# Attention numerator of a linear-attention and Fourier-mixing kernel: whole-array products on head-major features in place of products on column halves

## The chip, the cores and the metric

The kernel runs on one core of a Trainium2 chip. The metric is the device time of one execution in microseconds, as the median of several runs. The profile is of one execution of its own; its times start at the first instruction of that execution.

## The reference: what is computed

There are two blocks. The first is an attention with random features, over 8 batches, 8 heads, 576 positions and a head size of 64, with 128 features. For each batch and head:

```
phi(x) = exp(h - max(h)) / sqrt(128),  h = x omega^T - |x|^2 / 2   (x scaled by 64^(-1/4))
kv = phi(k)^T v                 128 x 64
z  = sum over positions of phi(k)
num = phi(q) kv,   den = phi(q) z + 1e-6
attn = num / den                576 x 64
```

The heads are joined to rows of 512. The second block adds to these rows x the real part of a two-dimensional Fourier transform over positions and columns, u = x + Re(FFT2(x)), normalizes each row of u, and returns u + relu(un w_ch1) w_ch2 with a hidden size of 2048. The two weight matrices arrive as 64-bit floats.

## The kernel before, in words

**Tiling of the attention.** Heads are taken in pairs, so there are 32 pairs (8 batches by 4). The 576 positions of a head are 64 x 9: partition p and chunk r (R = 9 chunks) hold position 9p + r. One tile thus has 128 partitions, 64 for each head of the pair. `attn` (from L407) does a pair:

- it transposes nine 128 x 128 tiles of k and q together (`transposed`, L354, tile `kqT`), and forms the projections `pp` (L433);
- `softmax` (L382) takes the maximum over features on VectorE (L387) and the exponential on ScalarE (L399). The resulting feature tiles `e` have (head, position) on partitions;
- `kvp` (L455) is the sum over nine chunks of features of k by v, with a column of ones for the denominator, so that each head has 65 columns. VectorE copies it to `kv` (L467);
- the features of q are transposed in the groups of chunks (0), (1 to 4), (5 to 8), each into one PSUM bank, and ScalarE copies each group to the tile `qeT` (L378): 128 features on partitions, and for each chunk 128 columns, head 0's 64 positions and then head 1's. The copy of the last group reads each 128 columns backwards, which also swaps the heads in them;
- the numerator products write `ndp`, two PSUM banks: 65 columns for each of four slots in the first bank (head 0), and for four slots and two more in the second (head 1, and chunk 0 of both heads). Each of the slots holds two chunks: the dictionary `SLOTS` (L28) says for chunks 1 to 8 which half of the output partitions and which slot each takes. A product at L496 has a stationary piece of 128 features by 64 positions and writes 64 output partitions, so that it uses a column half of TensorE's array. The two products at L504 have 128 stationary columns, of which the first 64 outputs are used later;
- VectorE adds a small number to the denominators (L517), takes reciprocals (L520) and multiplies (L527) into the batch's tile `x`.

The rest of a batch is `mix` (folds on VectorE L552 to L566, transforms `yp` L591 and `ab` L618 and L623 on TensorE), then norms, and for four row tiles the plain two-layer product `plain_of` (`hp` L799, `op` L822), while the weights are converted to 32 bit (`narrow`). These are interleaved with the attention. After that, eight blocks of 512 rows go through a fast matrix multiplication with seven products (`first_of` L953, `second_of` L1043).

**What sets the order of the work.** Everything is written as streams of steps (`Step`: engine, planned microseconds, what it waits for, buffers taken and given). `Listing.run` simulates the streams with these planned costs and issues the instructions of a step when it is the earliest that can start. The order of instructions on each engine is therefore fixed when the kernel is built, and the planned costs shape it. The numerator's step on TensorE is planned at 1.5 us, takes two of eight PSUM banks, waits for `kv` and all three copies of `qeT`, and gives back `qeT` and `kv`. The VectorE step after it gives back the two banks.

Of the kernel before, what the change touches and what calls it, by code (L numbers as in the profile page):

```python
# [13 lines left out]
AF = mybir.ActivationFunctionType  # L14
ALU = mybir.AluOpType
AX = mybir.AxisListType
F32 = mybir.dt.float32
# [7 lines left out]

SLOTS = {1: (0, 0), 2: (1, 0), 3: (0, 1), 4: (1, 1), 8: (0, 2), 7: (1, 2), 6: (0, 3), 5: (1, 3)}  # L28
SLOTS[0] = (0, 4)
NL = 2  # L30
NC3 = NL + 1

# [1 line left out]
PE, ACT, DVE, POOL, SP, NONE = "pe", "act", "dve", "pool", "sp", "none"  # L34
# [128 lines left out]
def kernel(  # L163
# [10 lines left out]
    nc = tc.nc  # L174

    B, H, S, D = q.shape
# [12 lines left out]
    P = 128  # L189

    R = S // 64
# [32 lines left out]
    att = early.enter_context(tc.tile_pool(name="att", bufs=NS))  # L224
# [4 lines left out]
        bank=8, kq=NKQ, turned=NS, e=NE, e1=NS, kv=NS, x0=1, x1=1, fold=1, half=1, y=1,  # L229
# [3 lines left out]
    def bank(name):  # L233
        return psum.tile([128, 512], F32, name=name, tag="bank")
# [116 lines left out]
            rows = slice(D * i, D * i + D)  # L351
            nc.vector.tensor_scalar(om2[rows, i, :], omps[rows, 0:128], SCALE, None, op0=ALU.mult)

    def transposed(src, name, groups, after, makes, give, back=None):  # L354


        dst = None
        for j0, j1 in groups:
            m = j1 - j0
            yield Step(  # L360
                PE,
                0.11 * m,
                after=after(j0, j1),
                take=("bank",) + (("turned",) if j0 == 0 else ()),
                give=give(j0, j1),
            )
            if dst is None:
                dst = att.tile([128, R, 128], F32, name=name, tag="turned")
            ps = bank("tps")
            for j in range(j0, j1):  # L370
                nc.tensor.transpose(ps[:, (j - j0) * 128 : (j - j0 + 1) * 128], src(j), ident[:])  # L371
            yield Fork(evicted(dst, ps, j0, j1, makes, (j0, j1) == back))
        return dst

    def evicted(dst, ps, j0, j1, makes, back):
        yield Step(ACT, 0.15 + 0.115 * (j1 - j0), 0.1, makes=makes + (j0,), give=("bank",))
        ps = ps[:, 0 : 128 * (j1 - j0)].rearrange("q (c p) -> q c p", p=128)
        nc.scalar.activation(  # L378
            out=dst[:, j0:j1, :], in_=ps[:, :, ::-1] if back else ps, func=AF.Copy
        )  # L380

    def softmax(n, t, num, ps, es):  # L382

# [23 lines left out]
    def attn(n):  # L407
        b, pr = divmod(n, NP)

        yield Step(NONE, after=(("kq", n), "om2") + ((("vd", n - 1),) if n else ()))  # L410
        kq = kqs.pop(n)

        flat = kq[:].rearrange("p c d -> p (c d)")
        kqT = yield from transposed(
            lambda j: flat[:, 128 * j : 128 * j + 128],
            "kqT",
            ((0, 4), (4, 8), (8, R)),
            lambda j0, j1: (),
            ("kqT", n),
            lambda j0, j1: ("kq",) if j1 == R else (),  # L420
        )
        es = {}
        for t, num in enumerate((4, 4, 4, 4, 2)):
            yield Step(
                PE,
                0.215 * num,
                after=(("kqT", n, 2 * t // 4 * 4),),
                take=("bank",),
                give=("turned",) if num == 2 else (),
            )  # L430
            ps = bank("pp")
            for j in range(num // 2):
                nc.tensor.matmul(  # L433
                    ps[:, 256 * j : 256 * j + 256],
                    lhsT=kqT[:, 2 * t + j, :],
                    rhs=om2[:].rearrange("p i m -> p (i m)"),
                )
            yield Fork(softmax(n, t, num, ps, es))

        def feature(c):  # L440
            return es[c // 4][:, c % 4, :]

        kvp = None
        for r0, r1 in ((0, 4), (4, 8), (8, R)):
            yield Step(
                PE,
                0.225 * (r1 - r0),
                after=(("e", n, r0 // 4),) + (("vd", n),),
                take=("bank",) if r0 == 0 else (),
                give=("e" if r1 < R else f"vd{n % NV}",),  # L450
            )
            if kvp is None:
                kvp = bank("kvp")
            for r in range(r0, r1):
                nc.tensor.matmul(  # L455
                    kvp[:, 0 : 2 * (D + 1)],
                    lhsT=feature(r),
                    rhs=vds[n % NV][:, r, :],
                    start=(r == 0),
                    stop=(r == R - 1),  # L460
                )
        kvs = []

        def keep():
            yield Step(DVE, 0.3, take=("kv",), give=("bank",), makes=("kv", n))
            kv = att.tile([128, 2, D + 1], F32, name="kv", tag="kv")
            nc.vector.tensor_copy(  # L467
                out=kv[:].rearrange("m i d -> m (i d)"), in_=kvp[:, 0 : 2 * (D + 1)]
            )
            kvs.append(kv)  # L470

        yield Fork(keep())

        qeT = yield from transposed(
            lambda r: feature(R + r),
            "qeT",
            ((0, 1), (1, 5), (5, R)),
            lambda j0, j1: tuple(("e", n, t) for t in range((R + j0) // 4, (R + j1 - 1) // 4 + 1)),
            ("qeT", n),
            lambda j0, j1: {1: (), 5: ("e",), R: ("e", "e1")}[j1],  # L480
            (5, R),
        )
        yield Step(
            PE,
            1.5,
            after=(("kv", n), ("qeT", n, 0), ("qeT", n, 1), ("qeT", n, 5)),
            take=("bank", "bank"),
            give=("turned", "kv"),
        )
        ndp = [bank("ndp"), bank("ndp")]  # L490

        for i, order in enumerate(((2, 1, 4, 3, 7, 8, 5, 6), (2, 1, 4, 3, 7, 8, 5, 6))):
            for r in order:
                g, slot = SLOTS[r]
                c0 = D * (1 - i if r >= 5 else i)
                nc.tensor.matmul(  # L496
                    ndp[i][D * g : D * g + D, (D + 1) * slot : (D + 1) * (slot + 1)],
                    lhsT=qeT[:, r, c0 : c0 + D],
                    rhs=kvs[0][:, i, :],
                )  # L500

        flat = qeT[:].rearrange("q c p -> q (c p)")
        for i in range(2):
            nc.tensor.matmul(  # L504
                ndp[1][:, (D + 1) * (4 + i) : (D + 1) * (5 + i)],
                lhsT=flat[:, D * i : D * i + P],
                rhs=kvs[0][:, i, :],
            )
        yield Step(DVE, 1.8, after=(("frame", b),), give=("bank", "bank"), makes=("x", b, pr))
        x = xts[b % 2]  # L510
        rden = small.tile([P, 10], F32, name="rden", tag="rden")
        nds = [
            t[:, 0 : (D + 1) * n].rearrange("p (c d) -> p c d", d=D + 1)
            for t, n in zip(ndp, (4, 6))
        ]
        for i, n in enumerate((4, 6)):
            nc.vector.tensor_scalar(  # L517
                rden[:, 4 * i : 4 * i + n], nds[i][:, :, D], DEN_EPS, None, op0=ALU.add
            )
        nc.vector.reciprocal(out=rden[:], in_=rden[:])  # L520
        cols = x[:, :, 2 * D * pr : 2 * D * (pr + 1)].rearrange("p c (i d) -> p c i d", i=2)
        for p1, dst, nd, den in (
            (P, cols[:, 0:4, 0], nds[0], rden[:, 0:4]),
            (P, cols[:, 0:4, 1], nds[1][:, 0:4], rden[:, 4:8]),
            (64, cols[0:64, 4], nds[1][0:64, 4:6], rden[0:64, 8:10]),
        ):
            nc.vector.tensor_tensor(  # L527
                out=dst,
                in0=nd[:, :, 0:D],
                in1=den.unsqueeze(2).to_broadcast(list(dst.shape)),  # L530
                op=ALU.mult,
            )
# [341 lines left out]
    def pairs(start):  # L874
        for n in range(start, B * NP, NS):
            yield from attn(n)
# [24 lines left out]
        bank=8, slab=0, u=2, ht=NFC, hs=HF, ur=4, s=6, set=2,  # L901
# [241 lines left out]
```

## Time and profile before

| | |
|---|---|
| median of 3 runs | 1330.62 us (1330.33 to 1332.33) |
| the profiled execution | 1329.76 us, span of its instructions 1328.0 us |
| granted TensorE clock, mean | 0.995 |
| instructions | 20075, of which 7777 on TensorE |
| numerator products on column halves (L496) | 1024 MATMUL instructions, 28.5 to 454.0 us |
| numerator products on the whole array (L504) | 128 MATMUL instructions, 29.6 to 454.6 us |
| projections `pp` (L433) | 576 MATMUL instructions |
| copies to `qeT` (L378) | 96, median 592 ns |

A float32 product appears as two MATMUL instructions, each with a weight load (LDWEIGHTS, shown as PEld). "128*64" beside a matmul means 128 rows and 64 columns of the array in use, "128x65" its output of 65 columns in the moving direction. Lengths of matmuls overlap, so that the difference of starts tells what one costs when many follow each other. In lines with "<-" the left side waits for the right one.

### The profile page before, as it was taken

The page shows a single profiled execution, that of the slowest core. Times are in us where ns is not written, and L with a number is a line of the kernel's source. Part 1 is how long each engine was busy: PE and PEld are TensorE (multiplying, and loading weights), DVE is VectorE, ACT ScalarE, POOL GpSimd, SP SyncE. Part 2 cuts the span into 40 slices and gives each one's busy share as a digit, 9 for nine tenths or more (in the row PEclk, how much of TensorE's full clock was granted, in tenths as well). Part 3 has the DMA queues.
Part 4 walks back from the last instruction along what each step waited for, and adds up shares of the span by engine and source line. Part 5 has one row for each costly group of instructions (what it writes and reads, how often), then busy time and mean ns, then how long its engine had stood idle before and what let it go on. Part 6 is the DMA issues. An engine that isn't in the chain of part 4 may idle for free.

```text
span 1328.0 us, 20075 instructions
## 1 busy us (share of the span) xinstructions
PE 1302.6 (98%) x7777; PEld 1135.3 (85%) x7777; DVE 558.1 (42%) x1347; ACT 407.1 (31%) x1200; POOL 294.3 (22%) x407
## 2 busy tenths in 40 slices
PE   5999999999999999899999999999999999999998
PEld 5988988889989776788888888888888888888887
DVE  2788879897575620652132132132131231241211
ACT  4856666565655411210210210210210210210210
POOL 2213222321000010340330340340340330330420
PEclk8999999999999999999999999999999999999999
DMA  8535663554322120100200200200200201101101
GB/s 218 155 108 155 180 175 118 140 167 133 87 92 68 60 76 17 56 17 8 72 17 8 72 17 9 72 17 9 71 17 16 64 17 24 57 16 25 40 1 32
DMA packets 82464, 89.66 MB, mean 68 GB/s; under 512 B 42944, under 2 KB 51392, under 8 KB 82368
## 3 DMA queue, kind: packets, MB, share of 16 engines
q1 hardware_dynamic: 77760, 71.59, 20.0%
q0 software_dynamic: 4608, 16.78, 4.0%
q8 instruction: 62, 1.02, 0.3%
q14 instruction: 34, 0.28, 0.1%
HBM read 69.47 MB, written 23.07 MB: 70 GB/s over the span
## 4 chain that ended last, share of the span: by engine, by line
PE 95%; DMA 2%; DVE 2%; SPq 1%; issue 0%; ACT 0%; DVEq 0%
PE sx L1043 17%; PE sx L953 16%; PE pp L433 8%; PE sz L1043 8%; PE sz L953 8%; PE kvp L455 5%; PE tps L371 4%; PE sy L1043 4%; PE sy L953 4%; PE op L822 4%; PE hp L799 4%; PE yp L591 4%; PE ndp L496 3%; PE ab L618 2%; PE ndp L504 1%; PE tp L738 1%
## 5 line engine op out<-in xcount | busy, mean ns | idle before, releaser
L399 ACT ACTIVATE e<-pp,nmx 128x128 f32<-128x128 f32 x576 | 157.2, 407 | 48.5 <-DVE nmx L387 48.4
L1017 POOL TENSOR_TENSOR hs<-ht,ht 128x256 f32<-128x256 f32 x64 | 47.9, 749 | 493.5 <-DVE ht L940 493.5
L967 ACT ACTIVATE s<-sx 128x256 f32<-128x256 f32 x128 | 48.9, 383 | 344.0 <-PE sx L953 326.7
L433 PE MATMUL pp<-om,kqT 128*128 128x256 f32 x576 | 136.3, 382 | 0.0
L953 PE MATMUL sx<-unT,w 128*128 128x256 f32 x512 | 131.2, 379 | 0.8 <-DVE ur L835 0.8
L433 PEld LDWEIGHTS pp<-om,kqT 128*128 128x128 f32 x576 | 106.0, 192 | 14.4 <-issue 1.2
L1043 PE MATMUL sx<-w,ht 128*128 128x256 f32 x512 | 114.4, 379 | 0.0
L953 PEld LDWEIGHTS sx<-unT,w 128*128 128x128 f32 x512 | 97.2, 190 | 14.7 <-DVE ur L835 1.6
L387 DVE TENSOR_REDUCE nmx<-pp 128x4 f32<-128x512 f32 (+1 forms) x160 | 95.9, 629 | 28.5 <-PE pp L433 20.7
L1043 PEld LDWEIGHTS sx<-w,ht 128*128 128x128 f32 x512 | 96.8, 190 | 12.8
L940 DVE CUSTOM_DVE_ANT_0 ht<-sz,s 128x256 f32<-128x256 f32 x64 | 27.1, 424 | 184.4 <-PE sz L953 184.4
L455 PE MATMUL kvp<-vd,e 128*128 128x130 f32 x576 | 77.0, 281 | 9.8 <-DMA vd<-in_v_dram 9.8
L1054 DVE TENSOR_TENSOR ur<-ur,sx 128x256 f32<-128x256 f32 x64 | 26.9, 421 | 140.1 <-PE sx L1043 140.1
L455 PEld LDWEIGHTS kvp<-vd,e 128*128 128x128 f32 x576 | 73.9, 195 | 12.7 <-issue 10.2
L319 POOL TENSOR_TENSOR w<-w,raw 128x512 f32<-128x512 f32 x32 | 47.0, 1475 | 163.6 <-DVE raw L317 154.7
L1000 ACT ACTIVATE ht<-sx 128x256 f32<-128x256 f32 x64 | 24.5, 383 | 172.3 <-PE sx L953 172.3
L953 PE MATMUL sz<-tt,w1s 128*128 128x256 f32 x256 | 65.6, 379 | 1.8 <-DVE w1s L925 1.8
L953 PE MATMUL sx<-tt,w 128*128 128x256 f32 x256 | 65.7, 380 | 1.0 <-DVE ht L940 1.0
L953 PE MATMUL sz<-unT,w1s 128*128 128x256 f32 x256 | 65.6, 379 | 0.0
L953 PE MATMUL sx<-tt,w1s 128*128 128x256 f32 x256 | 65.6, 379 | 0.0
L953 PE MATMUL sy<-unT,w 128*128 128x256 f32 x256 | 65.6, 379 | 0.0
L378 ACT ACTIVATE qeT<-tps 128x512 f32<-128x512 f32 (+1 forms) x96 | 44.9, 497 | 54.7 <-PE tps L371 54.4
(107 smaller groups left out, 2246.6 us busy)
## 6 DMA issues: line engine op xcount, KB each, us to landing
raw<-in_moe_w_ch_dram POOLq DMA_DIRECT2D x32, 512.0 KB, 6.2
kq<-in_k_dram SPq DMA_DIRECT2D x32, 288.0 KB, 2.9
kq<-in_q_dram SPq DMA_DIRECT2D x32, 288.0 KB, 3.8
vd<-in_v_dram SPq DMA_DIRECT2D x64, 144.0 KB, 4.4
out_dram<-ur SPq DMA_DIRECT2D x72, 128.0 KB, 2.4
u<-us SPq DMA_DIRECT2D x32, 256.0 KB, 4.3
ur<-us SPq DMA_DIRECT2D x32, 256.0 KB, 3.6
uh<-x SPq DMA_DIRECT2D x16, 256.0 KB, 3.5
```

Of the source, the lines that this page charges most:

```text
L371: nc.tensor.transpose(ps[:, (j - j0) * 128 : (j - j0 + 1) * 128], src(j), ident[:])
L387: nc.vector.tensor_reduce(nmx[:, 0:num], ps[:, 0 : MF * num].rearrange("p (c m) -> p c m", m=MF), axis=AX.X, op=ALU.max, negate=True,)
L399: nc.scalar.activation(out=e[:, c, :], in_=ps[:, MF * c : MF * c + MF], func=AF.Exp, bias=nmx[:, c : c + 1],)
L433: nc.tensor.matmul(ps[:, 256 * j : 256 * j + 256], lhsT=kqT[:, 2 * t + j, :], rhs=om2[:].rearrange("p i m -> p (i m)"),)
L455: nc.tensor.matmul(kvp[:, 0 : 2 * (D + 1)], lhsT=feature(r), rhs=vds[n % NV][:, r, :], start=(r == 0), stop=(r == R - 1),)
L591: nc.tensor.matmul(yp[:, 0:NK], lhsT=fold[:, c, n, :], rhs=tab[:, c, :], start=(c == 0), stop=(c == NC3 - 1),)
L799: nc.tensor.matmul(hp[:, 0:TP], lhsT=w1[:, dc, 128 * fc : 128 * fc + 128], rhs=unTs[key][:, dc, :], start=(dc == 0), stop=(dc == NDC - 1),)
L822: nc.tensor.matmul(yp[:, 0:DM], lhsT=hs[fc][:, 128 * i : 128 * i + 128], rhs=w2[:, fc, :], start=(fc == 0), stop=(fc == NFC - 1),)
L953: nc.tensor.matmul(ps[:, 0:HT], lhsT=left(dc), rhs=right(dc), start=start and dc == 0, stop=(dc == D2 - 1), skip_group_check=True,)
L967: nc.scalar.activation(out=s[:], in_=ps[:, 0:HT], func=AF.Copy)
L1017: nc.gpsimd.tensor_tensor(out=o, in0=l, in1=r, op=op)
L1043: nc.tensor.matmul(ps[:, 0:HM], lhsT=left(fc), rhs=right(fc), start=start and fc == 0, stop=(fc == HF - 1), skip_group_check=True,)
```

## The change

The dictionary `SLOTS` goes. The copies of the transposed q features put the two heads apart: `qeT` becomes a flat tile of 9 x 128 columns, first all nine chunks of head 0, then all nine of head 1, 64 columns each. In the last group the chunks are also written in reverse order (8 to 5), and the positions in each chunk of a head backwards. Then chunks 1 and 2 of one head, or 3 and 4, 8 and 7, 6 and 5, are 128 contiguous columns, and one product with 128 stationary columns writes a whole slot. For each head there are five products: four slots and chunk 0, the latter with 64 further columns that nobody reads. The 18 products of a pair become 10. The planned cost of the step goes from 1.5 to 1.36 us. The copy of the k and q tile is the same as before, written with flat indices.

```diff
-SLOTS = {1: (0, 0), 2: (1, 0), 3: (0, 1), 4: (1, 1), 8: (0, 2), 7: (1, 2), 6: (0, 3), 5: (1, 3)}
-SLOTS[0] = (0, 4)
...
-                dst = att.tile([128, R, 128], F32, name=name, tag="turned")
+                dst = att.tile([128, R * 128], F32, name=name, tag="turned")
...
-    def evicted(dst, ps, j0, j1, makes, back):
-        yield Step(ACT, 0.15 + 0.115 * (j1 - j0), 0.1, makes=makes + (j0,), give=("bank",))
-        ps = ps[:, 0 : 128 * (j1 - j0)].rearrange("q (c p) -> q c p", p=128)
-        nc.scalar.activation(
-            out=dst[:, j0:j1, :], in_=ps[:, :, ::-1] if back else ps, func=AF.Copy
-        )
+    def as_is(dst, ps, j0, j1):
+        return dst[:, 128 * j0 : 128 * j1], ps[:, 0 : 128 * (j1 - j0)]
+
+    def by_heads(dst, ps, j0, j1):
+
+        o = dst[:].rearrange("q (i c p) -> q c i p", i=2, p=D)[:, j0:j1]
+        i = ps[:, 0 : 128 * (j1 - j0)].rearrange("q (c i p) -> q c i p", i=2, p=D)
+        return o, i[:, ::-1, :, ::-1] if j0 > 2 * NL else i
...
-                    lhsT=kqT[:, 2 * t + j, :],
+                    lhsT=kqT[:, 128 * (2 * t + j) : 128 * (2 * t + j + 1)],
...
-            1.5,
+            1.36,
...
-        for i, order in enumerate(((2, 1, 4, 3, 7, 8, 5, 6), (2, 1, 4, 3, 7, 8, 5, 6))):
-            for r in order:
-                g, slot = SLOTS[r]
-                c0 = D * (1 - i if r >= 5 else i)
+
+        for i in range(2):
+            for slot in range(5):
+                c0 = D * (R * i + (2 * slot + 1 if slot < 2 * NL else 0))
+                s0 = (D + 1) * (slot if slot < 2 * NL else slot + i)
                 nc.tensor.matmul(
-                    ndp[i][D * g : D * g + D, (D + 1) * slot : (D + 1) * (slot + 1)],
-                    lhsT=qeT[:, r, c0 : c0 + D],
+                    ndp[i if slot < 2 * NL else 1][:, s0 : s0 + D + 1],
+                    lhsT=qeT[:, c0 : c0 + P],
                     rhs=kvs[0][:, i, :],
                 )
-
-        flat = qeT[:].rearrange("q c p -> q (c p)")
-        for i in range(2):
-            nc.tensor.matmul(
-                ndp[1][:, (D + 1) * (4 + i) : (D + 1) * (5 + i)],
-                lhsT=flat[:, D * i : D * i + P],
-                rhs=kvs[0][:, i, :],
-            )
```

More of the change, by code (lines that the diff above doesn't have):

```diff
@@ L352, in first, with transposed @@
             nc.vector.tensor_scalar(om2[rows, i, :], omps[rows, 0:128], SCALE, None, op0=ALU.mult)
-    def transposed(src, name, groups, after, makes, give, back=None):
+    def transposed(src, name, groups, after, makes, give, evicted):
         dst = None
@@ L371, in transposed, with kept @@
                 nc.tensor.transpose(ps[:, (j - j0) * 128 : (j - j0 + 1) * 128], src(j), ident[:])
-            yield Fork(evicted(dst, ps, j0, j1, makes, (j0, j1) == back))
-        return dst
-    def evicted(dst, ps, j0, j1, makes, back):
-        yield Step(ACT, 0.15 + 0.115 * (j1 - j0), 0.1, makes=makes + (j0,), give=("bank",))
-        ps = ps[:, 0 : 128 * (j1 - j0)].rearrange("q (c p) -> q c p", p=128)
-        nc.scalar.activation(
-            out=dst[:, j0:j1, :], in_=ps[:, :, ::-1] if back else ps, func=AF.Copy
-        )
+            def kept(j0=j0, j1=j1, ps=ps):
+                yield Step(
+                    ACT, 0.15 + 0.115 * (j1 - j0), 0.1, makes=makes + (j0,), give=("bank",)
+                )
+                o, i = evicted(dst, ps, j0, j1)
+                nc.scalar.activation(out=o, in_=i, func=AF.Copy)
+            yield Fork(kept())
+        return dst
+    def as_is(dst, ps, j0, j1):
[4 more added lines that the diff above has]
+        return o, i[:, ::-1, :, ::-1] if j0 > 2 * NL else i
     def softmax(n, t, num, ps, es):
@@ L420, in attn @@
             lambda j0, j1: ("kq",) if j1 == R else (),
+            as_is,
         )
@@ L480, in attn @@
             lambda j0, j1: {1: (), 5: ("e",), R: ("e", "e1")}[j1],
-            (5, R),
+            by_heads,
         )
```

## The prediction, made before the changed kernel ran

> **What bounds the kernel now.** I read the page's busy shares and slices first, then busy time by stage, then the timeline of TensorE around single numerator blocks, and last the waits.
>
> ```profile
> PE 1302.6 (98%) x7777; PEld 1135.3 (85%) x7777; DVE 558.1 (42%) x1347; ACT 407.1 (31%) x1200; POOL 294.3 (22%) x407
> ...
> PE   5999999999999999899999999999999999999998
> ...
> DVE  2788879897575620652132132132131231241211
> ```
>
> TensorE is the bound, and evenly so: after the first slice no slice falls under 8 tenths. The change touches only the attention, which runs from the first numerator product at 28.5 us to the last at 454.6 us. The stages:
>
> ```profile
> core 0: us, PE busy (x) PEld busy (x) DVE busy (x) ACT busy (x) POOL busy (x), PEclk, DMA share, GB/s
> 0.00:28.00 28.00, 14.11 (x69) 12.40 (x70) 5.16 (x11) 9.52 (x27) 7.79 (x23) 0.82 0.91 223
> 28.00:456.00 428.00, 424.71 (x3600) 376.34 (x3598) 326.21 (x814) 270.34 (x850) 86.36 (x95) 1.00 0.46 129
> 456.00:1328.00 872.00, 863.79 (x4112) 746.54 (x4110) 226.74 (x524) 127.23 (x324) 200.14 (x289) 1.00 0.12 32
> ```
>
> In the attention's stage TensorE has 3.3 us free of 428, at full granted clock; VectorE has 102 us free and ScalarE 158 us. So what a numerator block takes on TensorE is paid on the path almost one for one. One such block, with its neighbours:
>
> ```profile
> 107.67 1.06 PE L799 MATMUL hp<-unT,w 128*128 128x128 f32 x8
> 108.65 1.15 PE L496 MATMUL ndp<-kv,qeT 128*64 128x65 f32 x32
> 109.74 0.66 PE L504 MATMUL ndp<-kv,qeT 128*128 128x65 f32 x4
> 110.23 1.00 PE L799 MATMUL hp<-unT,w 128*128 128x128 f32 x7
> ```
>
> The columns are start, length, line, tiles, shape and count. A product of float32 is two MATMUL instructions here: 16 products on column halves give x32, the two whole-array ones give x4. What counts is start to start, not the length of one, since matmuls overlap. Two narrower windows give the spacings that the merged rows hide: the last `hp` before the block, and the last three of L504.
>
> ```profile
> 108.45 0.28 PE L799 MATMUL hp<-unT,w 128*128 128x128 f32 x1
> ...
> 109.90 0.50 PE L504 MATMUL ndp<-kv,qeT 128*128 128x65 f32 x3
> ```
>
> From the last `hp` at 108.45 to the next one at 110.23 are 1.78 us. Eight `hp` from 107.67 to 108.45 are seven spacings of 0.112 us; without its own spacing, the block costs 1.78 − 0.11 = 1.67 us. It splits so: entry into column halves 0.09 us over the normal spacing (108.45 to 108.65 is 0.20); 32 instructions from 108.65 to 109.74, among which the switch back to the whole array is hidden; then (110.23 − 109.90)/3 = 0.11 us for each whole-array one. Inside the halves the instructions start in pairs, a pair every 0.058 us (the trace's starts), so 32 take 16 × 0.058 = 0.93 us, and 1.09 − 0.93 = 0.16 us more go at its two ends; a further 0.05 us falls after the first instruction of L504 (1.67 − 0.09 − 0.93 − 0.16 − 4 × 0.11). The trace gives 1.67 us for nearly every block, whatever ran before it.
>
> **What the Trainium skill says.** "TensorE: Matmul & The Clock Gate", section "LDWEIGHTS (loading the stationary operand)", prices a weight load by its columns, P/1.2 ns: an estimate of 107 ns for 128 columns and 53 ns for 64. The trace agrees: 112 ns between whole-array instructions of 65 moving columns, 58 ns between pairs of half-array ones. The strongest witness is a product with almost nothing to stream, the one-column products of L623:
>
> ```profile
> 81.36 0.70 PE L623 MATMUL ab<-mid,cs_sb 128*128 128x1 f32 x5
> 81.92 0.69 PE L618 MATMUL ab<-cd_sb,y 128*128 128x129 f32 x4
> ```
>
> Five of them take 81.92 − 81.36 = 0.56 us, 0.112 each, as much as with 65 or 128 moving columns. The floor is the load of 128 weight columns.
> "TensorEngine Tiling (Array Packing)", section "Key Properties", says that a change of tiling mode drains TensorE, and that tiles load and multiply in parallel. Both show: 0.09 + 0.16 + 0.05 = 0.30 us a block lie around the two switches, and the halves' instructions start in pairs 7 ns apart. I found nothing there that prices an ACTIVATE with a strided output.
>
> **The change, part by part.**
> *Removed:* 16 half-array products (32 instructions) and both mode switches, in each of 32 pairs. With the two whole-array products the old block is 1.67 us, as above: 0.09 + 0.93 + 0.16 + 0.05 + 4 × 0.11 = 1.67.
> *Added:* 10 whole-array products with 65 moving columns, so 20 instructions. Each loads 128 weight columns, like L504 now, from a contiguous piece of `qeT`, and streams the same right side. At 0.112 us: 20 × 0.112 = 2.24 us, no switch before or after. So +0.57 us a pair, and 32 × 0.57 = **+18.2 us** on TensorE. Fewer instructions, but the halves loaded two sets of 64 columns at once, in the time of one; now the 128 columns of the same two chunks pass one after the other.
> Three kinds of instruction with 128 weight columns (L504, L623, L799) show this pace, within 2 ns, so 32 × 20 × 0.002 = 1.3 us either way.
> *The eviction.* The Copy on ScalarE now writes runs of 64 at two places half a tile apart; its reversed read was there before. The forward group and the reversed one take 597 and 592 ns now, and the copy into `kqT`, unchanged in its data, 607 on average. No row shows a copy with this output. Lower bound: a gain of some ns, since the reversed read is cut finer, not excluded; upper bound: each of 64 copies doubled, +38 us for ScalarE, which leaves it 120 of its 158 us of room and makes the third copy 0.6 us later, which after the lateness below would cost TensorE some 0.6 us in four pairs and less in four more, about 3 us. I take nothing; the cover is that the third copy ends about 1 us before the block starts in most pairs (only in four after, by 0.01, 0.35, 0.43 and 0.94 us).
> *Order of the products.* Now the block opens with chunks 2 and 1 and asks for the last copy 8 instructions later; the new one asks for it at its third product, 4 instructions in, and if waits are kept for the span of the strided write, at its first. That can add at most the lateness above in those four pairs, about 1.7 us in all; I take 0.5. Behind the waiting product stand all of TensorE's later instructions. The waits now:
>
> ```profile
> PEld ndp L496 <- ACT qeT L378: 1.8, 4, 0.8
> ```
>
> *VectorE.* It waits at the first `rden` for `ndp` [0], which is complete after 8 × 0.112 = 0.90 us where 16 × 0.029 = 0.46 us stood, and at the second for the block's end, 0.57 us later. Behind it stand the divisions, maxima of the next `pp` and folds. TensorE's following work moves by the same 0.57 us, so the relative lateness stays. Cost nothing, covered by 102 us of idle VectorE; in the dense stage around 200 to 300 us (92 of 100 us busy) six blocks × 0.57 = 3.4 us could come back as TensorE waits.
> *What absorbs it.* TensorE waits for folds for 3.0 us in all (three times, 1.9 the longest). A later TensorE could hide up to that. VectorE's fold depends on the `x` of the same blocks and moves too, in part; I take half, −1.5 us.
> *The planner.* The step's cost goes from 1.5 to 1.36 us, which is farther from the 2.24 us expected; the order of issue on every engine, SP's and POOL's DMAs included, may shuffle. TensorE, being late against plan, finds its inputs ready. I take nothing and keep ±4 us, about the 3.3 us of idle there now. The product stages after 456 us are not touched.
>
> **Sum:** 18.2 + 0.5 − 1.5 = +17.2 us. Against its own execution: 1329.76 with a span of 1328.0 (1.8 us around it) becomes 1347.0; the median of the runs is 0.86 us higher, 1330.62, so I predict 1347.8.
>
> **Rivals.**
> *The new waits add up:* the lateness of copies (1.7), VectorE's hold (3.4) and a worse order (some 2): 18.2 + 7 = +25 us, 1356. For it: VectorE's 92% between 200 and 300 us. Against: TensorE gets slower, so the others gain room.
> *Absorbed:* all of the fold waits go and the new order happens to be 4 us better: 18.2 − 3 − 4 = +11 us, 1342. Against: only 3.3 us are free in the stage.
> *Faster:* the whole-array products run at the pace of the stream instead of the weight load, as half-array pairs do at 0.058 us for the same 65 columns. Then a block is 20 × 0.058 = 1.16 us, 0.51 less, and 32 blocks give −16.4 us, 1314. It decides at 1.67/20 = 0.084 us an instruction: below that the change gains. For it: a switch stands before the only four such instructions. Against: the spacing after the switch's effect, and L623 far from any switch.
> *No change:* a pace near 0.084 us; nothing in the trace shows one. That the edit is not what it says I see no way: the 8 half pairs become 8 whole products.
>
> **Chances.** Forecast 0.74 (own range 1344 to 1352), waits added 0.10, absorbed 0.10, faster 0.04, no change 0.02. Range 1342 to 1354: it takes in both ends of planner and waits and leaves out the gain. A measurement here tells about 0.2% from no change. Slower 0.94, same 0.02, faster 0.04.
>
> **What would show it.** In the changed profile: 640 instructions of one kind, 128*128 128x65, 0.112 us start to start; no 128*64 `ndp`; blocks of 2.24 us; fold waits smaller; `qeT` copies near 0.6 us. Spacings under 0.084 us, or over 5 us of new TensorE waits, would make it wrong.

## The result, and the profile after

The changed kernel takes 1345.03 us (median of 4 runs, 1344.74 to 1345.85) against 1330.73 before (four runs; the 1330.62 above is the median of three): +14.3 us. The ratio is 1.0106, with a 95% interval of 1.0089 to 1.0124. The profiled execution took 1345.03 us with a span of 1343.2, against 1329.76 and 1328.0: between the two traces there are 15.2 us to explain.

The busy shares and TensorE's slices on the page of the changed kernel:

```profile
PE 1320.6 (98%) x7265; PEld 1159.7 (86%) x7265; DVE 556.7 (41%) x1344; ACT 409.3 (30%) x1203; POOL 294.3 (22%) x407
...
PE   6999999999999999899999999999999999999998
```

TensorE has 512 matmul instructions fewer (16 x 32, as 36 become 20 in each of 32 pairs) and is busy 18 us longer. The other engines are where they were. The chain of waits of the changed kernel is TensorE to 95%, as before. One kind of numerator product is left, of the 640 instructions that were forecast:

```profile
L505 PE MATMUL ndp<-kv,qeT 128*128 128x65 f32 x640 | 75.1, 273 | 0.2 <-ACT qeT L375 0.2
```

The stages, the second from 28 us to just past the last numerator product at 470.2 us:

```profile
core 0: us, PE busy (x) PEld busy (x) DVE busy (x) ACT busy (x) POOL busy (x), PEclk, DMA share, GB/s
28.00:470.00 442.00, 440.51 (x3078) 399.88 (x3078) 322.95 (x806) 271.94 (x852) 85.97 (x95) 1.00 0.45 125
470.00:1343.00 873.00, 864.96 (x4115) 746.61 (x4114) 227.87 (x527) 126.92 (x323) 200.52 (x289) 1.00 0.12 32
```

All of the new time lies in the attention: its last numerator product starts at 470.2 us instead of 454.6, and what follows keeps its 872 to 873 us. TensorE is freer of waits in it than before: 1.5 us idle instead of 3.3. One block in the timeline of TensorE, between two groups of `hp` like the one in the prediction:

```profile
156.25 1.06 PE L800 MATMUL hp<-unT,w 128*128 128x128 f32 x8
157.14 2.34 PE L505 MATMUL ndp<-kv,qeT 128*128 128x65 f32 x20
159.32 1.89 PE L800 MATMUL hp<-unT,w 128*128 128x128 f32 x15
```

Eight `hp` at 0.112 us are 0.89 us, which is all of 157.14 − 156.25: the entry is free now. The block is 159.32 − 157.14 = 2.18 us. In it the second instruction starts 0.057 us after the first and all others 0.112 us apart, 0.057 + 19 x 0.112 = 2.18. The next product's second instruction then starts 0.05 us later than usual (0.164 us for `hp`), which was so before the change as well. Counted from the last start before the block to the second start after it, without the normal spacings of the neighbours, a block costs 1.72 us before and 2.23 us after, with the same value in nearly all blocks (where transposes follow, both are 0.05 us less). That is +0.51 us, and 32 x 0.51 = +16.3 us. This full count is used below for every kernel.

What TensorE waited for, in the changed kernel:

```profile
PE kvp L463 <- DMA vd<-in_v_dram: 8.5, 1, 8.5
...
PE tps L368 <- DMA kq<-in_k_dram: 1.3, 2, 1.1
...
PE tps L368 <- ACT e L406: 0.6, 2, 0.4
```

and before, where the waits for folds (the last line) are 3.0 us; they are gone after:

```profile
PE kvp L455 <- DMA vd<-in_v_dram: 9.8, 1, 9.8
...
PE yp L591 <- DVE fold L566: 3.0, 3, 1.9
```

### The profile page after: what moved, and what is told of

Read it like the earlier page. It is cut to its first block, busy times and chain, and to the rows that moved or that the text cites. A ratio compares the mean times of both kernels' runs of the same rounds, so it can differ in the third digit from the quotient of the medians.

```text
span 1343.2 us, 19066 instructions
## 1 busy us (share of the span) xinstructions
PE 1320.6 (98%) x7265; PEld 1159.7 (86%) x7265; DVE 556.7 (41%) x1344; ACT 409.3 (30%) x1203; POOL 294.3 (22%) x407
## 4 chain that ended last, share of the span: by engine, by line
PE 95%; DMA 2%; DVE 1%; ACT 0%; SPq 0%; issue 0%; DVEq 0%
PE sx L1044 16%; PE sx L954 16%; PE sz L1044 8%; PE pp L441 8%; PE sz L954 8%; PE ndp L505 5%; PE tps L368 5%; PE kvp L463 5%; PE hp L800 4%; PE op L823 4%; PE sy L1044 4%; PE sy L954 4%; PE yp L592 4%; PE ab L619 2%; PE tp L739 1%; PE ab L624 1%
## 5 line engine op out<-in xcount | busy, mean ns | idle before, releaser
L505 PEld LDWEIGHTS ndp<-kv,qeT 128*128 128x128 f32 x640 | 75.0, 192 | 2.0 <-issue 0.7
L505 PE MATMUL ndp<-kv,qeT 128*128 128x65 f32 x640 | 75.1, 273 | 0.2 <-ACT qeT L375 0.2
```

The source lines that it names most:

```text
L505: nc.tensor.matmul(ndp[i if slot < 2 * NL else 1][:, s0 : s0 + D + 1], lhsT=qeT[:, c0 : c0 + P], rhs=kvs[0][:, i, :],)
```

## The experiments

The kernel before was run again beside each of the two series of experiments, with a median of 1331.9 us in both. Differences in us between runs are the measured ratio times that. The profiled execution of before, at 1329.76 us, lies 2.1 us under this median, so a difference between two traces can come out some 2 us larger than the one between the runs.

**The layout alone.** The changed kernel with its head-major copies, the products on column halves again, the planned cost 1.5 us.

```diff
-            1.36,
+            1.5,
...
-            for slot in range(5):
...
+            for slot in range(2 * NL):
+                for g in range(2):
+                    c0 = D * (R * i + 2 * slot + 1 + g)
+                    nc.tensor.matmul(
+                        ndp[i][D * g : D * g + D, (D + 1) * slot : (D + 1) * (slot + 1)],
+                        lhsT=qeT[:, c0 : c0 + D],
+                        rhs=kvs[0][:, i, :],
+                    )
...
```

> The changed kernel's head-major layout and its copies, but the products on column halves and the planned cost 1.5 us as before (the two products of chunk 0 stay on the whole array). Theory (TensorE pays 128 weight columns for each whole-array instruction, all else is free): as before, 1330.7 us within 0.2%, copies of 512 columns at 0.59 to 0.60 us, numerator block 1.67 us. Rival (the strided copies cost, or make the products wait): 2 to 5 us slower, copies over 0.65 us or new waits of the products for the copies.

Measured: 1331.92 us, ratio to before 0.9998 (0.9987 to 1.0008). The copies to `qeT`, in the row of this tile (count, then shortest, median and longest time in ns):

```profile
L375 ACT ACTIVATE qeT<-tps x96: 272/594/641, 25.8 to 456.5; 128x512 f32<-128x512 f32 x64, 128x128 f32<-128x128 f32 x32
```

The median was 592 ns before. The layout and its copies cost nothing that can be measured; the change's loss lies in the products or in the plan.

**The plan alone.** The kernel before with the new planned cost.

```diff
-            1.5,
+            1.36,
```

> The kernel before with the planned cost 1.36 instead of 1.5 us and nothing else: the order of issue shuffles. Theory: within 3 us of 1330.7, block unchanged at 1.67 us. Rival (the new order moves the time): faster by 3 us or more, which would explain why the change cost 14.3 us and not the 16.3 that 32 x (2.18 - 1.67) gives; or slower by 3 or more.

Measured: 1331.15 us, ratio 0.9997 (0.9989 to 1.0005). The order of issue changes, and with it the waits, but not the time:

```profile
PE tps L371 <- DMA kq<-in_k_dram: 3.1, 3, 1.4
```

No wait for folds is left in this kernel, and TensorE waits for loads of `kq` instead. So part of the new pattern of waits in the changed kernel comes from the plan, not from the products. This kernel also has the planned costs of the changed one, so that the two issue in the same order: their spans are 1329.5 and 1343.2 us, 13.7 apart. TensorE's gaps between matmuls add up to 20.1 us in this kernel and 18.0 in the changed one; 16.3 − 2.1 = 14.2 us, and 0.5 us stays unexplained.

**The products with the old plan.** The changed kernel with 1.5 us planned.

```diff
-            1.36,
+            1.5,
```

> The changed kernel with the planned cost put back to 1.5 us. Theory: 1330.7 + 32 x 0.51 = 1347 us, less what is absorbed, so 1344 to 1348. Rival (order matters): outside that, below 1342 or above 1350.

Measured: 1344.1 us, ratio 1.0091 (1.0077 to 1.0106), +12.1 us. It has the planned costs of the kernel before, so the order is the same here too. In its waits:

```profile
PE kvp L463 <- DMA vd<-in_v_dram: 9.6, 1, 9.6
...
PE yp L592 <- DVE fold L567: 1.0, 3, 0.4
```

At equal order the blocks add 16.3 us and the fold waits fall from 3.0 to 1.0, which gives 14.3; the spans are 1342.0 against 1328.0, 14.0 apart. This is absorption seen alone: two of the three microseconds in which TensorE had waited for VectorE's folds are filled by the slower products. The plan being as before, the loss is the products'.

**Wider streams for head 0.** The changed kernel, where five of ten products stream 128 columns.

```diff
+                n = D + 1 if i else 2 * D
...
-                    ndp[i if slot < 2 * NL else 1][:, s0 : s0 + D + 1],
+                    ndp[i if slot < 2 * NL else 1][:, s0 : s0 + n],
...
-                    rhs=kvs[0][:, i, :],
+                    rhs=kvs[0][:].rearrange("m i d -> m (i d)")[:, (D + 1) * i : (D + 1) * i + n],
```

> The changed kernel, with the five products of head 0 streaming 128 columns instead of 65 (the further columns are written over or not read; the output is the same). Theory (the load of 128 weight columns sets the pace): at most 0.003 us on 10 instructions a pair, +1 us, 1346. Rival (the streamed columns set it): 63 more columns at 0.84 ns (216 ns for 256 columns in the product stage) on 320 instructions, 0.053 x 320 = +17 us, 1362.

Measured: 1344.91 us, ratio 1.0098 (1.0083 to 1.0113), the same as the changed kernel. A block in its timeline:

```profile
60.94 2.34 PE L506 MATMUL ndp<-kv,qeT 128*128 128x128 f32 x20
63.12 1.11 PE L463 MATMUL kvp<-vd,e 128*128 128x130 f32 x8
```

(The row merges both widths; there are ten of each.) 63.12 − 60.94 = 2.18 us, the same as with 65 columns throughout. The number of streamed columns, up to 128, doesn't enter the pace at all. What both widths have in common is the load of 128 weight columns. What half of them cost can be read in the kernel before, in the one-column products of `ab` (L623): those with 128 weight columns start 0.111 us apart, those with 64 start 0.058 us apart (medians of the trace's starts), though neither streams more than one column.

**No whole-array product.** The kernel before, with chunk 0 on column halves too. The filler pieces in the second half are not read.

```diff
-            nc.tensor.matmul(
-                ndp[1][:, (D + 1) * (4 + i) : (D + 1) * (5 + i)],
-                lhsT=flat[:, D * i : D * i + P],
-                rhs=kvs[0][:, i, :],
-            )
+            for g in range(2):
+                nc.tensor.matmul(
+                    ndp[1][D * g : D * g + D, (D + 1) * (4 + i) : (D + 1) * (5 + i)],
+                    lhsT=flat[:, D * (i + g) : D * (i + g) + D],
+                    rhs=kvs[0][:, i, :],
+                )
```

> The kernel before, with chunk 0 on column halves too: the two whole-array products become four half products (the second half of each pair is a piece nobody reads), so that no product of the block loads 128 columns. Theory: 4 x 0.112 us go and 4 pairs x 0.058 come, 0.22 us a pair less, 32 x 0.22 = -7 us: 1324, faster than both kernels. Rival (the work does not depend on the weight columns, only on the count of instructions, which goes from 36 to 40): 1331 or slower.

Measured: 1325.01 us (7 runs), ratio to before 0.9951 (0.9932 to 0.9970), −6.5 us. It beats both kernels, by going the opposite way. A block and its waits for folds:

```profile
108.28 1.15 PE L496 MATMUL ndp<-kv,qeT 128*64 128x65 f32 x32
109.27 0.40 PE L505 MATMUL ndp<-kv,qeT 128*64 128x65 f32 x8
109.60 1.16 PE L800 MATMUL hp<-unT,w 128*128 128x128 f32 x8
```
```profile
PE yp L592 <- DVE fold L567: 3.9, 3, 2.8
```

Forty instructions take 109.60 − 108.28 = 1.32 us, where 36 took 1.58 before and 20 take 2.18 after. In the full count a block is 1.51 us, so 32 x 0.21 = 6.8 us less, of which 0.9 us returns as longer fold waits. That leaves 5.9 us. The spans are only 4.4 us apart (1323.6 and 1328.0), because the first numerator product starts later in this trace, at 29.9 instead of 28.5 us; from there to the end it is 5.8 us shorter.

**The planned cost at its measured value.** The changed kernel, with 2.18 us planned.

```diff
-            1.36,
+            2.18,
```

> The changed kernel, with the planned cost at the measured 2.18 us. Theory: the order is worth little while TensorE is full, 1343 to 1348. Rival (the change was slow because the plan was wrong by 0.8 us a pair): clearly under 1342.

Measured: 1350.09 us, ratio 1.0138 (1.0120 to 1.0155): 5 us above the median of the changed kernel, or 4 us by the two ratios to before, and out of the range that was expected. The products are the same (2.18 us). TensorE's waits have new entries, and in one stage its clock fell:

```profile
PE tp L739 <- DVE u L735: 1.5, 1, 1.5
...
PE tps L368 <- ACT e L406: 0.7, 1, 0.7
PE ndp L505 <- DVE kv L475: 0.4, 1, 0.4
```
```profile
100.00:200.00 100.00, 98.93 (x705) 92.47 (x705) 87.43 (x203) 63.85 (x196) 37.28 (x38) 0.97 0.61 169
```

In the changed kernel that stage has 1.00. The trace gives one stretch of 6.8 us at half rate there, which costs 3.4 us; TensorE's gaps add up to 19.6 us against 18.0, another 1.7. These two sums make the 5 us between the two traces. They do not settle the runs: one of the four had a mean clock of 0.996, as the changed kernel has, and still took 1349.62 us. So how much of the loss is the clock's stays open. But the plan's error was not what made the change slow, and a truer cost did not give a better order.

**Two switches a block.** The kernel before, with each whole-array product right after its head's half products.

```diff
+        flat = qeT[:].rearrange("q c p -> q (c p)")
         for i, order in enumerate(((2, 1, 4, 3, 7, 8, 5, 6), (2, 1, 4, 3, 7, 8, 5, 6))):
             for r in order:
...
-
-        flat = qeT[:].rearrange("q c p -> q (c p)")
-        for i in range(2):
             nc.tensor.matmul(
                 ndp[1][:, (D + 1) * (4 + i) : (D + 1) * (5 + i)],
...
```

> The kernel before, with each whole-array product of chunk 0 put right after the half products of its head, so that a block changes between halves and whole array twice instead of once; same products, same plan. Theory (a change there and back costs 0.09 + 0.16 + 0.05 = 0.30 us, of which up to 0.06 is a pair's normal start): 32 x 0.24 to 0.30 = +8 to +10 us, 1339 to 1341. Rival (switches are free): 1331.

Measured: 1338.29 us, ratio 1.0046 (1.0034 to 1.0059), +6.1 us. The full count of a block is 2.02 us, +0.29, so the price of a switch there and back was right. 32 x 0.29 = 9.3 us, and the fold waits fall from 3.0 to 1.7, which leaves 8.0; the spans are 7.9 us apart (1335.9 and 1328.0). The runs give less than the traces, as far as the trace of before lies under its median.

**One half at a time.** The kernel before, with four products for one half and then four for the other.

```diff
-        for i, order in enumerate(((2, 1, 4, 3, 7, 8, 5, 6), (2, 1, 4, 3, 7, 8, 5, 6))):
+        for i, order in enumerate(((1, 3, 8, 6, 2, 4, 7, 5), (1, 3, 8, 6, 2, 4, 7, 5))):
```

> The kernel before with the half products of a head in another order: four for the upper half of the output partitions, then four for the lower, instead of taking turns. Same products, same layout, same plan. Theory (the halves are cheap because two neighbours in the queue load and multiply at once): no neighbours differ, so 32 instructions at 0.058 us instead of 16 pairs, +0.9 us a pair, +30 us, 1360, more than the change itself cost. Rival (a half product is cheap in itself, or the queue reaches past four of them): 1331.

Measured: 1340.28 us, ratio 1.0068 (1.0051 to 1.0084), +9.1 us: between the two expectations. A block of it:

```profile
110.57 1.55 PE L496 MATMUL ndp<-kv,qeT 128*64 128x65 f32 x32
112.04 0.66 PE L504 MATMUL ndp<-kv,qeT 128*128 128x65 f32 x4
```

The 32 half products take 112.04 − 110.57 = 1.47 us, where 1.09 us stood before and 2.0 were expected. The starts in the trace show how: the second to fifth instructions start 0.058 us apart, and so do the last five; between them every eight instructions take five such steps, since some start only 2 to 6 ns after another. This fits a queue in which an instruction for one half starts beside the late ones of the other half, some four instructions back; the trace does not tell which half an instruction belongs to, so this reading is inferred. What is shown is that a half product is not cheap in itself: at the two ends of the block each instruction costs 0.058 us, the price of a pair, and as much as a one-column product with 64 weight columns.

## Why the prediction was right

The mechanism was right at each of its main steps, and the total was 3 us too high (+17.2 against +14.3).

- **The pace.** 0.112 us an instruction, held against the stream's 0.058: the trace after shows 0.112, and the wide streams show that the streamed columns do not matter. The rival "faster" needed a pace under 0.084 us. The Trainium skill's price of a weight load by its columns ("TensorE: Matmul & The Clock Gate", section "LDWEIGHTS (loading the stationary operand)", 107 ns for 128 columns as an estimate) stands 5 ns under the measured one.
- **The old block, mis-sized by 0.05 us.** The term "without its own spacing, the block costs 1.78 − 0.11 = 1.67 us" ended at the start of the next product and missed the 0.05 us that this product's second instruction loses; the new block was charged for all 20 spacings of 0.112, which is the full cost. In like terms it is 1.72 and 2.23 us, or 1.67 and 2.18: +0.51 a pair and +16.3 us, not +18.2. That is 1.9 us of the miss.
- **The switches.** Predicted at 0.30 us a block, measured at 0.29 when one more is put in. They are what the change saves, and they are less than half of what the products lose: 32 half instructions cost 0.93 us and the 16 whole ones in their place 16 x 0.112 = 1.79.
- **The copies, the waits for them and VectorE's hold.** The copies are unchanged (593 against 592 ns). The 0.5 us allowed for products that wait for the last copy did not show: 0.2 us on TensorE, as before. The prediction also misread the lateness: in the trace of before one block, not four, starts ahead of the end of its third copy, by 0.43 us, and after it is again one, by 0.43 us. VectorE's wait at `rden` rose from 28.8 to 41.1 us and delayed no product of TensorE that the waits show.
- **Absorption.** Half of the 3.0 us of fold waits was taken, 1.5. At the old order 2.0 us went (the experiment with the old plan); in the changed kernel all 3.0 are gone, but its own order brings short waits of the transposes in their place.
- **The planner.** It was taken at nothing, with 4 us either way, on the argument that a late TensorE finds its inputs ready. The plan alone moved the runs by under 1 us and the changed kernel ran within 2 us under both plans, 1.36 and 1.5. That it came out so was in part luck: with 2.18 us planned the same products took 1350.09 us.
- **The rest.** The forecast was set on 1330.62 us. The profiled execution of before was 0.9 us under its median and that of after on it, so the traces lie 15.2 us apart and the medians 14.3. The traces differ in the start too: TensorE waited 8.5 against 9.8 us for `vd`, and the first numerator product starts at 27.6 instead of 28.5 us. Counted from that product to the end, blocks and waits explain the pairs of equal order to 0.3 us: +14.6 against 14.3 us for the changed kernel with the old plan, −5.8 against −5.9 with halves alone. The changed kernel itself issues in another order than before; there it is +16.1 us against 16.3 of blocks less 1.8 of waits, and some 1.5 us stay open.

## What to carry to other kernels

Price a small product by what its instruction has to load: a float32 product with 128 stationary columns and at most 128 streamed ones takes two steps of 0.112 us whatever its width, and two column halves side by side take half of that for the same columns, at the 65 streamed here. Fewer and fuller instructions are not a gain when the weight load is the floor. Measure a block from the last start before it to the second start after it, in both kernels alike, or the fringes go to one side only.

## What was not expected of the hardware

- Half products of one half, queued four in a row, still overlap with those of the other half in good part: 1.47 us for 32 instructions, against 1.09 when they take turns.
- At the edges of a block of whole-array products with 65 streamed columns the spacing changes by about half of its 0.112 us: the first spacing in the block is 0.057 us, and the first one of the next product is longer by 0.05 us, unless that is a transpose (longer by 0.006 us).
- The runs of the kernel before scatter by 5 us (1329.38 to 1334.49 in one series of 27), and the granted clock goes with it at the two ends: the three slowest have a mean of 0.993, and none under 1330 has less than 0.995. In between it does not tell: runs at 0.995 took 1329.38 to 1333.23 us. The traces show stretches of 6.8 to 10.2 us at half rate near the start. The profiled run of the layout alone has one more of 6.8 us, from 201.1 us, while TensorE waited 3.3 us for a fold (until 202.2). The one in the kernel planned at 2.18 us began at 111.5 us, where TensorE had just waited 0.7 and 0.4 us only; what sets them off is not shown.
